# Loading the first 128 rows of w_out in one transfer, with two filler products fewer, in a fused attention and multiplicative-FFN kernel

## The chip, the cores and the metric

The kernel runs on one core of one Trainium2 chip. The metric is the device time of one execution in microseconds (us), as the median of several runs. A profile of one further execution is shown beside it. In the profile PE is TensorE (PEld its weight loads), DVE is VectorE, ACT is ScalarE, POOL is GpSimd and SP is SyncE, which issues nearly all DMAs here; L219 means line 219 of the kernel before.

## The reference, cut to what matters

```python
# attention: q, k, v are (8, 8, 576, 64) float32, g_norm is (64,)
kv  = einsum('bhsd,bhse->bhde', k, v)
out = einsum('bhsd,bhde->bhse', q, kv)
x   = out / sqrt(mean(out * out, -1) + 1e-6) * g_norm     # then to (4608, 512)
# FFN: w1, w2 (512, 1024), w3 (1024, 1024), w_out (1024, 512), all float64
a = x @ w1
b = x @ w2
h = a * b @ w3
y = h @ w_out                                             # (4608, 512) float32
```

The weights arrive as 64-bit floats. The kernel receives their bits as 64-bit integers and makes 32-bit floats of them on the chip.

## The kernel before

The last two matrix products are folded into one. Before any token is processed, the kernel computes w3 @ w_out (`w3o_sb`, 1024 by 512), so that the FFN ends in one product with `w3o_sb`. This fold is the first stage, about 78 us long, and the change lies in its first 14 us. After it, nine groups of 512 tokens go through attention, the two gates and the projection, with one level of a Strassen-Winograd scheme in the large products; the change does not touch that part.

**The fold.** It runs twice over eight chunks (`KF` = 8), once for each half of w3's rows. Chunk c consists of 128 columns of w3 (four blocks of 128 by 128 per half) and of the 128 rows of w_out that go with them. For each chunk PE turns the four blocks of w3 (`turn_w3`, L731, four 128x128 transposes into PSUM), ACT copies them to SBUF (L733), and `fold_chunk` (L747) adds four products of 128x128 by 128x512 to four PSUM banks. Every fp32 product appears in the profile as two records. For chunk 0 of the first half the products are split by columns of w_out: four products with columns 0 to 255, then, around the preparation of chunk 1, four with columns 256 to 511.

**Loads.** `load_next` (L212 to L239) loads one chunk into a tile `raw` of 1024 64-bit words per partition, 512 for w3 and 512 for w_out. There are four such tiles, and the first four chunks' loads are issued at the start, in order, on SP's queue. Chunk 0 is loaded in four DMAs of 256 KB each: two halves of w3 (two blocks each), then the two halves of w_out's columns. Every later chunk takes two DMAs of 512 KB.

**Conversion.** `conversion` turns a stretch of `raw` into fp32 in six instructions: on ACT the absolute value of the high word (L176) and the low word (L171), on DVE the sign (L181), the clamp (L185), the shift (L188) and the addition of both words (L193). Chunk 0 is converted in quarters of 256 words: quarters 0 and 1 are w3, quarters 2 and 3 are the two column halves of w_out. Chunk 1 is converted in halves of 512 words: first w3, then w_out. ACT and DVE work in the order in which this stage is written out (a manual schedule), and so do PE and SP; each engine waits in place for its operands.

**Filler products.** `keep_warm(n, small)` (L297 to L302) issues n products of 128x128 and `small` products of 16x16 of the identity matrix into a PSUM bank that nobody reads. It is called three times: `keep_warm(11)` at the very start, `keep_warm(1, 12)` between the turn of chunk 0 and its products, and `keep_warm(1, 13)` between the last product of chunk 0 and the first of chunk 1:

```python
            if c == 0:
                fold_chunk(0, c, range(NH), slice(0, N))
                fold_chunk(0, c, range(NH - 1), slice(N, DM))
                begin_next(lambda: turn_w3(0, 1))
                fold_chunk(0, c, [NH - 1], slice(N, DM))
                keep_warm(1, 13)
                continue
```

**Semaphores of the DMAs.** The DMAs share eight completion semaphores in turn, so a DMA that reuses one waits on its issuing queue until the DMA eight places earlier has landed. Two of the eight are first taken by the two small loads of g_norm on ACT's queue.

Of the kernel before, what the change touches and what calls it, by code (L numbers as in the profile page):

```python
# [22 lines left out]
def kernel(  # L23
# [37 lines left out]
    DM = H * D  # L61
# [23 lines left out]
    def bank(pool, tag):  # L85
        return pool.tile([P, 512], FP32, name=tag, tag=tag)
# [6 lines left out]
    def load_q(b, r):  # L93
        t = loaded["q", b, r] = inp.tile([P, 2, J * D], FP32, name="q_sb")
        nc.sync.dma_start(
            out=t, in_=q[b, 2 * r:2 * r + 2, 0:G, :].rearrange("h (p j) d -> p h (j d)", j=J)
        )

    def load_four(names, b, g):

        for name in names:
            t = loaded[name, b, g] = inp.tile([P, 2, JS * D], FP32, name=f"{name}_sb", bufs=1)
            src = dict(k=k, v=v)[name][b, 4 * g:4 * g + 4]
            src = src.rearrange("(r e) (p j) d -> (e p) r (j d)", e=2, j=JS)
            nc.sync.dma_start(out=t, in_=src)

    def load_q_left(b):
        if b % 2 == 0:
            q_left[b // 2] = inp.tile([P, H, D], FP32, name="ql_sb", bufs=1)
        nc.sync.dma_start(  # L110
            out=q_left[b // 2][(b % 2) * L:(b % 2 + 1) * L],
            in_=q[b, :, G:S, :].rearrange("h p d -> p h d"),
        )
# [95 lines left out]
    def raw_tile():  # L209
        return conv_pool.tile([P, 1024], w1.dtype, name="raw", bufs=RAW)  # L210

    def load_next():  # L212
        if len(raws) == len(todo):
            return
        what, i = todo[len(raws)]
        raw = raw_tile()

        def load(where, src):
            nc.sync.dma_start(out=raw[:, where].rearrange("p (c m) -> p c m", c=src.shape[1]), in_=src)  # L219

        if what == "w":
            for n, w in enumerate((w1, w2)):
                src = w[:, i * P:(i + 1) * P].rearrange("(c p) f -> p c f", p=P)
                load(slice(n * 512, (n + 1) * 512), src)
        elif what == "b":
            for h in range(2):
                src = w3[DF // 2:DF, (2 * i + h) * P:(2 * i + h + 1) * P]
                load(slice(h * 512, (h + 1) * 512), src.rearrange("(m p) f -> p m f", p=P))
        else:
            src = w3[0:DF // 2, i * P:(i + 1) * P].rearrange("(m p) f -> p m f", p=P)  # L230
            cols = w_out[i * P:(i + 1) * P, :].rearrange("p (c f) -> p c f", c=1)

            n = 1 if i else 2
            for h in range(n):
                load(slice(h * 512 // n, (h + 1) * 512 // n), src[:, h * NH // n:(h + 1) * NH // n, :])
            for h in range(n):
                f = slice(h * DM // n, (h + 1) * DM // n)
                load(slice(512 + f.start, 512 + f.stop), cols[:, :, f])
        raws.append(raw)  # L239

    converted = []
# [22 lines left out]
    def begin_next(between=None, at=1):  # L264

        if len(begun) < len(todo):
            begun.append(conversions(len(begun)))
            for n, (c, _) in enumerate((c, i) for c in begun[-1] for i in range(2)):
                if between is not None and n == at:
                    between()  # L270
                next(c)

    def end_next(load=True):
        for c in begun[len(converted)]:
            all_of(c)
        converted.append(len(converted))
        if load:
            load_next()
# [18 lines left out]
    def keep_warm(n, small=0):  # L297

        t = bank(ps_mm, "mm")
        for i in range(n + small):  # L300
            w = P if i < n else 16
            nc.tensor.matmul(t[0:w, 0:w], lhsT=ident[:, 0:w], rhs=ident[:, 0:w], start=True, stop=True)  # L302
# [424 lines left out]
    def turn_w3(half, c):  # L727
        t_ps = bank(ps_at, "at").rearrange("p (m f) -> p m f", m=NH)
        for m in range(NH):
            src = chunks[:, c, 0, m * P:(m + 1) * P]  # L730
            nc.tensor.transpose(t_ps[:, m, :], src, ident)  # L731

        nc.scalar.copy(place_w3(half, c), t_ps)  # L733
# [9 lines left out]
    def fold_chunk(half, c, ms, cols=slice(0, DM)):  # L743
        if c == 0 and 0 in ms and cols.start == 0:
            sums_ps[half] = [bank(ps_mm, "mm") for m in range(NH)]
        for m in ms:
            nc.tensor.matmul(  # L747
                sums_ps[half][m][:, cols], lhsT=w3T[half, c][:, m, :], rhs=chunks[:, c, 1, cols],
                start=(c == 0 and cols.start == 0), stop=(c == KF - 1),
                skip_group_check=(half == 0),  # L750
            )
            if c == KF - 1:
                nc.scalar.copy(w3o_sb[:, half * NH + m, :], sums_ps[half][m])
# [693 lines left out]
    with tc.manual_schedule(  # L1447
        engines={mybir.EngineType.DVE, mybir.EngineType.Activation, mybir.EngineType.SP}
    ):
        for _ in range(RAW):  # L1450
            load_next()
# [25 lines left out]
        for c in range(KF):  # L1477

            if c > 3:
                begin_next()  # L1480
            end_next()
            if c == 4:
                load_four("k", 0, 0)
                load_q(0, 0)
            elif c == 5:
                load_four("v", 0, 0)
                load_q(0, 1)
                load_q_left(0)
            if c == 0:
                fold_chunk(0, c, range(NH), slice(0, N))  # L1490
                fold_chunk(0, c, range(NH - 1), slice(N, DM))
                begin_next(lambda: turn_w3(0, 1))
                fold_chunk(0, c, [NH - 1], slice(N, DM))
                keep_warm(1, 13)
                continue
            cut = NH - 1 if c in (1, 5) else NH - 2
            fold_chunk(0, c, range(cut))
            if c < 4:
                begin_next(lambda: turn_w3(0, c + 1), 2)
            else:  # L1500
                turn_w3(*((0, c + 1) if c + 1 < KF else (1, 0)))
            fold_chunk(0, c, range(cut, NH))
# [8 lines left out]
        for c in range(KF):  # L1511
# [9 lines left out]
            if c < KF - 2:  # L1521
                if c + 1 < max(BEGIN):
                    begin_next()
                elif c < max(BEGIN):
                    begun.append(conversions(len(begun)))
                    for steps_of_w in begun[-1]:
                        next(steps_of_w)
                if c == max(BEGIN) + 1:
                    for steps_of_w in begun[len(converted)]:
                        next(steps_of_w)  # L1530
                    all_of(x_first)
                else:
                    end_next(False)
                if c in SPLIT:
                    t = turns[SPLIT[c]] = w3_by_dma(SPLIT[c])
                    next(t)
                    next(t)
                if len(raws) < FIRST:
                    load_next()
                if c == 2:  # L1540
                    for steps_of_w in begun[len(converted)]:
                        next(steps_of_w)
                elif c == max(BEGIN):
                    run(sum_w(0))
            elif c == KF - 2:
                end_next(False)
# [211 lines left out]
```

## Time and profile before

| | before |
|---|---|
| time, median of 3 runs | 738.72 us (738.55 to 739.32) |
| the profiled execution, its own time | 738.91 us |
| its span, first to last instruction | 736.8 us |
| PE busy | 731.3 us (99%) |
| DVE busy | 627.5 us (85%) |
| ACT busy | 381.1 us (52%) |
| granted TensorE clock | 1.00 |
| HBM read, written | 130.55 MB, 20.71 MB |

The time of an execution is the span and some 2 us around it. PE is busy nearly throughout, but the page's busy time of PE is modelled and covers waits inside a pipelined stream, so the time that an edit is worth must be read from the stage in which it lies, from the chain of waits and from the order of instructions there.

### The profile page before, as it was taken

The page shows a single profiled execution, that of the slowest core. Times are in us where ns is not written, and L with a number is a line of the kernel's source. Part 1 is how long each engine was busy: PE and PEld are TensorE (multiplying, and loading weights), DVE is VectorE, ACT ScalarE, POOL GpSimd, SP SyncE. Part 2 cuts the span into 40 slices and gives each one's busy share as a digit, 9 for nine tenths or more (in the row PEclk, how much of TensorE's full clock was granted, in tenths as well). Part 3 has the DMA queues.
Part 4 walks back from the last instruction along what each step waited for, and adds up shares of the span by engine and source line. Part 5 has one row for each costly group of instructions (what it writes and reads, how often), then busy time and mean ns, then how long its engine had stood idle before and what let it go on. Part 6 is the DMA issues. An engine that isn't in the chain of part 4 may idle for free.

```text
span 736.8 us, 16930 instructions
## 1 busy us (share of the span) xinstructions
PE 731.3 (99%) x6873; PEld 658.4 (89%) x6873; DVE 627.5 (85%) x1259; ACT 381.1 (52%) x660; POOL 23.1 (3%) x30
## 2 busy tenths in 40 slices
PE   8999999999999999999999999999999999999998
PEld 6455788888899999999999999999999999999998
DVE  7988898868879689969996899689879987997797
ACT  7888778315652676167517761675177313212321
POOL 0000000220001000000010001000001000000000
PEclk9999999999999999999999999999999999999999
DMA  8999925599999598869987988698748862565454
GB/s 309 355 338 249 285 94 154 157 329 274 326 299 321 172 286 245 277 159 276 259 275 166 302 237 278 157 299 242 253 115 217 221 209 87 187 214 158 135 196 142
DMA packets 138769, 170.44 MB, mean 231 GB/s; under 512 B 81220, under 2 KB 114116, under 8 KB 138692
## 3 DMA queue, kind: packets, MB, share of 16 engines
q1 hardware_dynamic: 136240, 155.02, 71.4%
q10 hardware_dynamic: 2452, 14.35, 5.8%
q8 instruction: 54, 0.88, 0.5%
q14 instruction: 23, 0.19, 0.1%
HBM read 130.55 MB, written 20.71 MB: 205 GB/s over the span
## 4 chain that ended last, share of the span: by engine, by line
PE 98%; DMA 1%; DVE 0%; SPq 0%; issue 0%; ACT 0%; DVEq 0%
PE mm L778 37%; PE mm L1330 23%; PE mm L1072 21%; PE mm L747 8%; PE at L778 3%; PE at L362 3%; PE mm L440 1%; PE at L440 1%; PE at L731 1%; DMA raw<-in_moe_w_out_dram 1%; PE at L1373 0%; PE at L459 0%; PE at L382 0%; PE mm L302 0%; SPq L219 0%; PE at L476 0%
## 5 line engine op out<-in xcount | busy, mean ns | idle before, releaser
L1121 ACT COPY slots<-mm 128x512 f32<-128x512 f32 x88 | 51.6, 586 | 127.3 <-PE mm L1330 83.1
L778 PE MATMUL mm<-xT,w_sb 128*128 128x256 f32 x432 | 99.3, 379 | 0.0
L778 PEld LDWEIGHTS mm<-xT,w_sb 128*128 128x128 f32 x432 | 81.4, 190 | 11.1 <-issue 0.5
L778 PE MATMUL mm<-xc,ws 128*128 128x256 f32 x328 | 74.4, 379 | 0.0
L778 PEld LDWEIGHTS mm<-xc,ws 128*128 128x128 f32 x328 | 62.3, 190 | 8.5
L796 ACT COPY slots<-mm 128x512 f32<-128x512 f32 x58 | 34.0, 585 | 69.5 <-PE mm L778 64.7
L747 PE MATMUL mm<-chunks,ab 128*128 128x512 f32 (+1 forms) x136 | 59.2, 573 | 0.3 <-DVE chunks L193 0.3
L1125 DVE TENSOR_TENSOR slots<-mm,slots 128x512 f32<-128x512 f32 x66 | 45.2, 685 | 16.3 <-PE mm L1072 15.9
L1122 ACT COPY slots<-mm 128x384 f32<-128x384 f32 x88 | 42.3, 481 | 25.0 <-PE mm L1330 22.1
L1072 PE MATMUL mm<-ws,w3o_sb 128*128 128x128 f32 x350 | 54.0, 275 | 0.0
L1330 PE MATMUL mm<-w3o_sb,ab 128*128 128x128 f32 x368 | 48.8, 276 | 0.0
L408 DVE TENSOR_REDUCE inv<-sq 128x8 f32<-128x512 f32 (+1 forms) x40 | 24.6, 629 | 26.9 <-ACT sq L407 26.9
L1072 PEld LDWEIGHTS mm<-ws,w3o_sb 128*128 128x128 f32 x350 | 46.4, 192 | 0.0
L1330 PEld LDWEIGHTS mm<-w3o_sb,ab 128*128 128x128 f32 x368 | 45.4, 192 | 0.5
L1330 PE MATMUL mm<-w3o_sb,raw 128*128 128x128 f32 x340 | 43.5, 275 | 0.0
L747 PEld LDWEIGHTS mm<-chunks,ab 128*128 128x128 f32 x136 | 24.0, 190 | 21.0 <-issue 17.9
L1330 PEld LDWEIGHTS mm<-w3o_sb,raw 128*128 128x128 f32 x340 | 40.7, 192 | 0.0
L778 PE MATMUL mm<-xT,ws 128*128 128x256 f32 x160 | 38.1, 381 | 0.0
L1126 DVE TENSOR_TENSOR slots<-mm,slots 128x384 f32<-128x384 f32 x66 | 36.3, 551 | 2.0 <-PE mm L1330 1.9
L778 PE MATMUL mm<-xc,w_sb 128*128 128x256 f32 x152 | 36.6, 384 | 0.0
L778 PEld LDWEIGHTS mm<-xT,ws 128*128 128x128 f32 x160 | 30.1, 190 | 4.3 <-ACT slots L796 0.2
L335 ACT COPY xT<-xn 128x1024 uint16<-128x1024 uint16 x26 | 30.2, 1167 | 3.5 <-DMA xn<-xT 3.5
(247 smaller groups left out, 1664.3 us busy)
## 6 DMA issues: line engine op xcount, KB each, us to landing
w3o_sb<-w_l SPq DMA_DIRECT2D x21, 896.0 KB, 6.2
w3o_sb<-w3o_l SPq DMA_DIRECT2D x18, 896.0 KB, 6.6
raw<-in_moe_w_dram SPq DMA_DIRECT2D x31, 512.0 KB, 7.8
raw<-w3o_l SPq DMA_DIRECT2D x15, 896.0 KB, 4.9
w3o_sb<-w3o_l ACTq DMA_DIRECT2D x14, 896.0 KB, 4.8
k_sb<-in_k_dram SPq DMA_DIRECT2D x16, 576.0 KB, 4.9
v_sb<-in_v_dram SPq DMA_DIRECT2D x16, 576.0 KB, 5.8
q_sb<-in_q_dram SPq DMA_DIRECT2D x32, 256.0 KB, 5.4
```

What stands on the lines that cost most here:

```text
L335: copy(words(dst), src)
L362: nc.tensor.matmul(ps[r * D:(r + 1) * D, :], lhsT=k_sb[rows, r, cols], rhs=v_sb[rows, r, cols], start=(j == 0), stop=(j == JS - 1),)
L408: adds["norm"] = nc.vector.tensor_reduce(out=inv[:, i], in_=sq.rearrange("p (h d) -> p h d", d=D), axis=AX.X, op=ALU.add)
L747: nc.tensor.matmul(sums_ps[half][m][:, cols], lhsT=w3T[half, c][:, m, :], rhs=chunks[:, c, 1, cols], start=(c == 0 and cols.start == 0), s ...
L778: nc.tensor.matmul(ps[:, u, :], lhsT=lhsT(a_name, u, c), rhs=rhs(b_name, c),  start=(u == 0 and c == 0 and new), stop=(c == chunks - 1), s ...
L796: copies.setdefault(name, []).append(nc.scalar.copy(t, ps))
L1072: nc.tensor.matmul(ps[place // 4][:, place % 4, :], lhsT=x, rhs=y, start=new and place // 4 not in seen, stop=True, skip_group_check=True,)
L1121: nc.scalar.copy(z[:, 0:4], ps[0])
L1122: return nc.scalar.copy(z[:, 4:7], ps[1][:, 0:3])
L1125: nc.vector.tensor_add(z[:, 0:4], ps[0], z[:, 0:4])
L1126: nc.vector.tensor_add(z[:, 4:7], ps[1][:, 0:3], z[:, 4:7])
L1330: nc.tensor.matmul(ps[place // 4][:, place % 4, :], lhsT=x[:, c, :], rhs=y[:, c, :], start=new and place // 4 not in seen, stop=(c == 1), ...
```

## The change

The load of chunk 0 still splits w3 in two, but brings w_out's 128 rows in one DMA of 512 KB, whole rows of 512 words, instead of two DMAs of 256 KB with half of each row. The last of the three `keep_warm` calls issues 11 small products instead of 13. The conversion of chunk 0 stays in quarters. Quarters 2 and 3 now both depend on the one DMA, so the separate DMA waits of ACT and DVE for quarter 3 are gone. One DMA fewer also moves every later DMA of this start by one place in the round of eight semaphores. Otherwise the instructions of each engine and their order are the same.

```diff
             n = 1 if i else 2
             for h in range(n):
                 load(slice(h * 512 // n, (h + 1) * 512 // n), src[:, h * NH // n:(h + 1) * NH // n, :])
-            for h in range(n):
-                f = slice(h * DM // n, (h + 1) * DM // n)
-                load(slice(512 + f.start, 512 + f.stop), cols[:, :, f])
+            load(slice(512, 1024), cols)
         raws.append(raw)
...
                 begin_next(lambda: turn_w3(0, 1))
                 fold_chunk(0, c, [NH - 1], slice(N, DM))
-                keep_warm(1, 13)
+                keep_warm(1, 11)
                 continue
```

## The prediction

> **What bounds the kernel now.** I read the page first: PE is busy 731.3 of 736.8 us and carries 98% of the chain that ended last, while 1% of the chain is a DMA of w_out. Then I asked for the chain in order of time, over the first 80 us.
>
> ```profile
> 1.75 5.11 DMA raw<-in_moe_w_out_dram
> 6.86 0.02 issue
> 6.88 0.45 ACT chunks L176
> 7.34 0.02 issue
> 7.36 0.30 DVE chunks L185
> ...
> 8.12 0.44 DVE chunks L193
> 8.55 0.14 issue
> 8.69 3.26 PE mm L747 x14
> 11.95 0.56 PE at L731 x4
> 12.51 0.43 PE mm L747 x2
> 12.95 0.97 PE mm L302 x28
> 13.91 2.77 PE mm L747 x6
> ```
>
> The columns are start, duration and what carried the chain. Until 8.69 us the end of the kernel hangs on the first half of w_out (issued at 1.75, landed at 6.86) and on its conversion. From 8.69 us on it is PE all the way: the waits of PE after 13 us are an empty list. So nothing later absorbs a shift; what this start loses or gains by its first product of chunk 1, at 13.84 us, the end does too.
>
> Next, DVE's part of the timeline (start, duration, line), to see what stands between the landing and 13.84 us.
>
> ```profile
> 6.37 0.42 DVE L193 CUSTOM_DVE_ANT_0 chunks<-chunks,ab 128x512 uint16<-128x512 uint16 x1
> 6.88 0.32 DVE L181 TENSOR_SCALAR ab<-raw 128x256 uint16<-128x256 uint16 x1
> ...
> 9.41 0.43 DVE L193 CUSTOM_DVE_ANT_0 chunks<-chunks,ab 128x512 uint16<-128x512 uint16 x1
> 9.75 0.46 DVE L181 TENSOR_SCALAR ab<-raw 128x512 uint16<-128x512 uint16 x1
> ...
> 12.98 0.69 DVE L193 CUSTOM_DVE_ANT_0 chunks<-chunks,ab 128x1024 uint16<-128x1024 uint16 x1
> ```
>
> DVE starts quarter 2 when the half lands (6.88) and then runs through quarter 3 and both halves of chunk 1 with no wait on a DMA, until 13.67 (12.98 and 0.69). The first product of chunk 1 starts at 13.84, right behind that. So DVE, not the fillers on PE, paces this stretch, and a later 6.88 moves 13.67 by the same amount.
>
> Last, the DMA view for the one issue at 2.33 us, and the wait list of tile raw up to 9.1 us.
>
> ```profile
> raw<-in_moe_w_out_dram SPq DMA_DIRECT2D x1, 256.0 KB, 5.2
> ```
> ```profile
>   DMA raw<-in_moe_w_out_dram: 0.9, 1
> ```
>
> The first column of numbers is the count, then the size and the us to landing: the second half lands at 2.33 + 5.2, by the landing record at 7.57, which is 0.71 us after the first. ACT waited 0.9 us for w_out, once: for the first half alone. The second half is not read before 8.03 (ACT) and 8.46 (DVE), so it has 0.46 us to spare.
>
> **The change, part by part.**
>
> *One transfer for two.* Quarter 2 now waits for all 512 KB. The trace's packet records give 84 ns for a packet of 2048 bytes and 159 ns for one of 4096 (half a row and a whole row; the 4096 ones are chunk 1's). Each of the 16 DMA engines carries 8 of the 128 rows. An engine now does 8 x 84 = 0.67 us for the first half; for whole rows it does 8 x 159 = 1.27 us. If its first packet starts when it does now, each engine ends 0.60 us later, and the last lands at 6.86 + 0.60 = 7.46. From the other side: both halves are in at 7.57, and whole rows save 8 x (168 - 159) = 0.07, which gives 7.50. I take 7.46, +0.60 us. The outer bounds are far. Below, DVE is busy with quarter 1 until 6.79 (6.37 and 0.42), so even an instant landing gains 0.09. Above, chunk 1's w_out, of the same size and shape, took 7.1 us from issue to landing; from 1.75 that is 8.85, +2.0. That row has 512 KB of chunk 1's w3 packed right ahead of it in the same rings, so I stay near the two halves' own rows.
>
> A rule of the Trainium skill can be weighed here (DMA: Bandwidth & Descriptors, "Rules for kernel authors"): coalesce many small transfers into one large one, since each pays a fixed cost, about 2 us by that page. Halves paying it in turn would be over 2 us apart; the trace's 0.71 us between their landings shows the cost overlapped, so by the trace there is nothing of it to save on the path.
>
> *What follows the landing.* Quarter 2's four DVE steps, quarter 3's four and chunk 1's eight keep their order, and move by 0.60. ACT has slack: its first step of chunk 1 waited 0.18 us for a DMA at 9.04, so ACT moves by only about 0.4 there. Chunk 1's loads (landed at 9.02 and 10.39 by the records) are not late, being issued earlier. PE's first product goes from 8.69 to 9.29, and the first of chunk 1 from 13.84 to 14.44.
>
> *One issue fewer on SP.* An issue is about 0.5 us of SP's time; the transfers behind it start that much sooner, or wait for another semaphore of the round. Chunk 2's w_out stood at 5.13 and chunk 3's w3 at 6.88 for reuse; in their new places they can go at about 3.8 and 5.13. Chunk 3's w_out, at 7.30 now, must wait for the one transfer, about 7.5. The DMA engines are over 0.9 busy from 6 us on and PE waits for none of these loads, so I cost this at nothing. If the cover were gone, 0.2 us of delay would be the price.
>
> *Two products fewer.* The 26 records of 16x16 start 25 ns apart, two records to a product, so two products are 0.10 us of PE. But the last filler starts at 13.735, DVE ends at 13.67 and the product starts at 13.84; the same hand-over at 8.54 to 8.69 took 0.15 us, so DVE alone would allow 13.82. The gain is 0.02 us, at most 0.10 if PE and not DVE set that start, as the chain has it. I take 0.02.
>
> Sum: +0.60 - 0.02 = +0.58 us. On the profiled execution, 738.91 (span 736.8 and 2.1 around it), that is 739.49. That execution is 0.19 above the median 738.72, from which it would be 739.30. I say 739.4. About 0.2%, or 1.48 us, is what a measurement of this kernel can tell from no change: my forecast lies well inside it.
>
> **The rivals.**
>
> *The transfer is no later than the half (no change, or a hair faster).* Between 3.75 and 4.75 us the DMA engines carry only some 200 GB/s against 375 to 400 later: some stand idle between the halves. One long transfer could fill these holes. Against it: the last engine sets the landing, and the records show that engine's two halves 0.71 apart, without a hole between. The gain is capped at 0.09 + 0.10 = 0.19 us: 738.5 to 738.9. Chance 0.16. That the split does nothing already is excluded: ACT went at 6.88, before the second half's 7.57.
>
> *TensorE's clock falls in the longer gap (slower).* PE now idles from 8.35 to 8.69 behind the fillers, and 0.85 us before 6.85. The first gap becomes 0.94 us, so between 6 and 9.3 us PE would have little but 16x16 products. If the clock were halved for half of the 3.26 us of products at 8.69, they would take 1.6 us more: with the 0.58, 740.9 from the median, and 742.6 if for all of them. It decides from the point where so thin a stretch counts as idle. For it: the fillers are the only PE work there. Against it: the granted clock reads 1.00 in every window that I asked for, through the 0.85 us gap too. The Trainium skill (TensorE: Matmul & The Clock Gate, "Why this matters for your kernels") wants no idle gap over about 3 us; by that rule 0.94 us leaves the clock alone, and no gap here is long enough to test it. Chance 0.10.
>
> *The whole transfer lands as late as chunk 1's row (slower).* At 7.1 us from issue to landing the shift would be +2.0 and the time 740.7. It needs an engine to get its share of descriptors later than it does now. Only a shift over 1.5 us passes the bound. Chance 0.09.
>
> **How the numbers follow.** The forecast, a shift of 0.3 to 1.1 us, has 0.60; its own range is 739.0 to 739.8. The rivals have 0.16, 0.10 and 0.09, and 0.05 is for what I don't see, split between the sides. Slower by over 0.2%: 0.10 + 0.09 and some of the rest and of the spread of the runs (0.8 us between the three shown), 0.23. Faster by over 0.2% has no mechanism, since the cap is 0.19 us: 0.04. Within: 0.73. The range starts at 738.4, below the capped gain, and ends at 740.9, at the near ends of both slower rivals.
>
> **What would show it.** Right: ACT's L176 of quarter 2 waits for w_out until about 7.5 instead of 6.88; DVE's L193 of chunk 1 ends near 14.27; PE's first 128x512 product follows at about 14.42; from there all is the same, shifted. The 16x16 records fall by four and the product after them still follows DVE. Wrong: quarter 2 starting near 6.9 (first rival), a granted clock under 1.00 in the first 20 us, or products at 8.69 over 379 ns each (second), or w_out landing after 8.3 (third). A shift at 14 us that the end does not show would break the reading that nothing later absorbs it.

## The result, and the profile after

| | before | after |
|---|---|---|
| median of 22 runs each | 738.59 us (738.09 to 739.56) | 741.06 us (738.79 to 742.83) |
| ratio to before | | 1.0026 (95% interval 1.0018 to 1.0034) |
| profiled execution, its span | 738.91 us, 736.8 | 741.13 us, 739.1 |

The changed kernel is slower by 0.26%, with an interval that lies wholly above 1. (The two medians alone give 1.0033; with two groups a median is unsteady, so I go by the ratio and its interval.) Its executions scatter over 4 us where those of before stay within 1.5. They form two groups, and the granted clock of TensorE tells most of them apart: in 12 of the 22 it reads 1.000, with a median of 739.74 us, and in 10 it reads 0.995 to 0.998, with a median of 741.25. Two of the twelve took 741.06 and 741.29 us all the same; neither was profiled, so why they are that long is not shown. The median of all, 741.06, lies at the lower edge of the second group and just above the top of the predicted range (by the ratio it would be 740.5, inside); my forecast of 739.4 is near the first.

The profiled execution is of the second group. This is its chain of waits, the answer to the one shown of before (L745 is before's L747, L729 is L731, L300 is L302):

```profile
1.75 6.52 DMA raw<-in_moe_w_out_dram
8.28 0.02 issue
8.30 0.44 ACT chunks L176
...
9.53 0.43 DVE chunks L193
9.96 0.14 issue
10.10 4.65 PE mm L745 x14
14.75 0.44 PE at L729 x4
15.19 0.43 PE mm L745 x2
15.62 0.87 PE mm L300 x24
16.48 2.77 PE mm L745 x6
```

Two things are longer. The transfer lands at 8.28 us, where in the kernel before the first half of w_out landed at 6.86: +1.42. And the 14 records of chunk 0's products take 4.65 us instead of 3.26: +1.39. The rest is what it was, less 0.10 for the fillers and 0.12 for the turn of chunk 1. So the first product of chunk 1 is 2.57 us late (13.91 to 16.48), and the span is 2.3 us longer.

DVE in the timeline (start, duration, line; the idle time before an instruction and what ended it in brackets), and the times that readers of tile raw waited for w_out up to 10.3 us (us in total, times):

```profile
6.27 0.42 DVE L193 CUSTOM_DVE_ANT_0 chunks<-chunks,ab 128x512 uint16<-128x512 uint16 x1
8.30 0.32 DVE L181 TENSOR_SCALAR ab<-raw 128x256 uint16<-128x256 uint16 x1 [1.61 <-DMA raw<-in_moe_w_out_dram]
...
14.38 0.69 DVE L193 CUSTOM_DVE_ANT_0 chunks<-chunks,ab 128x1024 uint16<-128x1024 uint16 x1
```
```profile
  DMA raw<-in_moe_w_out_dram: 4.1, 2
```

DVE now stands idle for 1.61 us before quarter 2, where it had 0.09. Its last step for chunk 1's w_out ends at 15.07 (14.38 and 0.69), 1.40 later than before. But the product starts only at 16.41, so in this execution PE and no longer DVE sets the pace there. With the hand-over of 0.15 us that before showed, DVE would have let it start at about 15.2 (an estimate). So of the 2.57 us some 1.4 belong to the landing and some 1.2 to PE. PE in the timeline, around its wait for w_out:

```profile
8.03 0.22 PE L1473 MATMUL at<-ident,g_row 1*128 1x1 f32 x1
10.10 4.65 PE L745 MATMUL mm<-chunks,ab 128*128 128x256 f32 x14 [1.84 <-DVE chunks L193]
```

Why is PE slow after that wait? The windows of this trace give, for stretches in us, the length, then busy time and instructions of PE, PEld, DVE, ACT and POOL, then the granted clock, DMA share and GB/s:

```profile
6.09:9.51 3.42, 1.95 (x33) 1.47 (x32) 1.37 (x5) 1.21 (x4) 0.00 (x0) 1.00 0.99 357
9.51:12.92 3.41, 2.82 (x7) 2.32 (x8) 3.05 (x9) 3.41 (x9) 0.00 (x0) 0.50 1.07 388
12.92:16.33 3.41, 3.41 (x39) 2.99 (x37) 3.19 (x8) 1.40 (x3) 0.00 (x0) 1.00 1.06 376
```

For 3.41 us, from 9.51 to 12.92, the clock is 0.50. These are the edges of the trace's own clock records. In the stretch of the same length before it lies the larger part of PE's wait for w_out, 1.26 of 1.84 us: its products end at 8.25 and start again at 10.10.

### The profile page after: what moved, and what is told of

Read it like the earlier page. It is cut to its first block, busy times and chain, and to the rows that moved or that the text cites. A ratio compares the mean times of both kernels' runs of the same rounds, so it can differ in the third digit from the quotient of the medians.

```text
span 739.1 us, 16920 instructions
## 1 busy us (share of the span) xinstructions
PE 732.8 (99%) x6869; PEld 660.6 (89%) x6869; DVE 629.0 (85%) x1259; ACT 380.4 (51%) x660; POOL 22.8 (3%) x30
## 4 chain that ended last, share of the span: by engine, by line
PE 98%; DMA 1%; DVE 0%; SPq 0%; issue 0%; ACT 0%; DVEq 0%
PE mm L776 37%; PE mm L1328 23%; PE mm L1070 21%; PE mm L745 8%; PE at L776 3%; PE at L360 3%; PE mm L438 1%; PE at L438 1%; DMA raw<-in_moe_w_out_dram 1%; PE at L729 1%; PE at L1371 0%; PE at L457 0%; PE at L380 0%; SPq L219 0%; PE at L474 0%; PE mm L300 0%
## 5 line engine op out<-in xcount | busy, mean ns | idle before, releaser
L745 PE MATMUL mm<-chunks,ab 128*128 128x512 f32 (+1 forms) x136 | 60.6, 586 | 1.8 <-DVE chunks L193 1.8
L745 PEld LDWEIGHTS mm<-chunks,ab 128*128 128x128 f32 x136 | 25.1, 198 | 22.8 <-issue 17.9
```

What stands on the lines that cost most here:

```text
L745: nc.tensor.matmul(sums_ps[half][m][:, cols], lhsT=w3T[half, c][:, m, :], rhs=chunks[:, c, 1, cols], start=(c == 0 and cols.start == 0), s ...
```

## The experiments

Each of the twelve was timed in 10 to 12 runs, with before beside it on the same chip, in four batches on three chips. Before's medians beside them were 738.73 (first four), 738.88 (next four), 738.64 (next two) and 738.70 us (last two). "Low" counts executions with a granted clock of 0.998 or less; of the 110 executions of before that were run beside these kernels none was low.

| kernel | median, us | ratio (95% interval) | low | median of the rest | of the low |
|---|---|---|---|---|---|
| the change | 741.06 | 1.0026 (1.0018 to 1.0034) | 10 of 22 | 739.74 | 741.25 |
| load alone | 740.91 | 1.0030 (1.0020 to 1.0041) | 6 of 10 | 739.92 | 741.96 |
| fillers alone | 738.83 | 1.0003 (0.9994 to 1.0012) | 0 of 11 | 738.83 | |
| change, more fillers | 740.12 | 1.0016 (1.0007 to 1.0025) | 0 of 11 | 740.12 | |
| halves swapped | 739.29 | 1.0008 (0.9999 to 1.0017) | 1 of 11 | 739.27 | 740.75 |
| two row halves | 740.84 | 1.0025 (1.0017 to 1.0034) | 6 of 11 | 740.26 | 741.26 |
| change, touch | 740.95 | 1.0029 (1.0018 to 1.0039) | 5 of 10 | 740.35 | 742.41 |
| before, touch | 739.24 | 1.0001 (0.9992 to 1.0010) | 0 of 11 | 739.24 | |
| before, no fillers | 738.71 | 0.9998 (0.9989 to 1.0006) | 2 of 11 | 738.69 | 740.40 |
| one transfer, 2 KB packets | 740.91 | 1.0021 (1.0012 to 1.0031) | 7 of 12 | 739.68 | 741.24 |
| w3 half by ACT | 738.84 | 1.0002 (0.9994 to 1.0011) | 0 of 11 | 738.84 | |
| w_out half by ACT | 739.76 | 1.0017 (1.0007 to 1.0028) | 5 of 12 | 739.47 | 741.36 |
| w_out whole by ACT | 741.24 | 1.0026 (1.0015 to 1.0037) | 7 of 11 | 739.54 | 742.05 |

**Which part of the change.** The load alone:

```diff
-                keep_warm(1, 11)
+                keep_warm(1, 13)
```

> The whole-row load alone, with the 13 fillers of before. Theory A (late landing of the whole transfer, and in part of the executions a fall of TensorE's clock in the gap that this makes): as the full change, 739.1 to 739.8 us where the clock stays at 1.000 and about 741.2 where it reads under 1.000, median 739.5 to 741.3. Rival B (the two fillers fewer thin out PE's work and let the clock fall): with 13 fillers the clock stays at 1.000 and the time is 738.7 to 739.8.

And the two fillers alone, on the kernel before:

```diff
-                keep_warm(1, 13)
+                keep_warm(1, 11)
```

> Two fillers fewer alone, w_out in halves as before. Theory A: no change, 738.5 to 738.7 us, clock 1.000 in all runs. Rival B: the clock under 1.000 in a good part of the runs and those some 1.5 us longer. If PE and not DVE set the first product of chunk 1: 0.10 us less, too little to be told.

The load alone does what the change does: 740.91 us, 6 of 10 low. The fillers alone do nothing that can be told, and none of their 11 executions was low. So the effect is that of the load, and the fall of the clock does not need the two fillers to be gone.

**Is it the clock, or only the landing?** The change, with five more 128x128 fillers where PE waits for w_out:

```diff
-        keep_warm(1, 12)
+        keep_warm(6, 12)
```

> The full change, with six instead of one 128x128 filler in the call ahead of chunk 0's products, about 1.1 us more of PE work in the gap. Theory A: the clock stays at 1.000 in all or nearly all runs, the part of the loss that goes with the clock is gone and the part that goes with the landing stays: median 739.3 to 740.0 us, and no run group around 741.2 with a lower clock. Rival (all of the loss is the late landing, the lower clock is hidden behind DVE): the same as the full change, about 741 us.

No execution was low, and the high group at 741.2 is gone: 740.12 us. In its trace w_out landed as late as with the change (8.12 us by the landing record), and the windows show a full clock:

```profile
6.06:9.47 3.41, 2.57 (x34) 2.21 (x34) 2.03 (x7) 1.75 (x6) 0.00 (x0) 1.00 1.00 353
9.47:12.88 3.41, 3.41 (x30) 2.97 (x26) 3.07 (x9) 3.41 (x8) 0.00 (x0) 1.00 1.06 390
```

So the loss has two parts. The late landing costs about 1.1 to 1.4 us where the clock stays full: 739.74 against 738.59 for the change, 740.12 against 738.73 here. (The second figure may hold a little of the fillers themselves: in the trace they and the small turn of g_norm behind them keep PE until 9.98 us, and DVE's quarter 2 is ready at 9.80.) The executions with half clock are 1.5 us longer than the others (741.25 against 739.74); the profile puts 1.39 us more on the 14 records, of which about 1.2 reach the next chunk. The two groups were sorted by the clock after the runs, so part of the 1.5 may be a still later landing; the split is an estimate, that there are two parts is shown.

**What decides the fall of the clock.** Two looks at it. The kernel before, with a thinner stretch of PE and no change of the loads:

```diff
-        keep_warm(1, 12)
+        keep_warm(1, 0)
```

> The kernel before, without the twelve 16x16 fillers in the call ahead of chunk 0's products; the loads are untouched. It makes the gap of PE ahead of 8.69 us about 1.3 us instead of 0.34 without any later landing. If a thin stretch of PE alone drops the clock: a good part of the runs reads under 1.000 and is 0.8 to 1.6 us longer than the rest, the rest at 738.7. If the 16x16 products do not count as work for the clock, or the fall needs more than 1.3 us: clock 1.000 and 738.5 to 738.8 us throughout.

Two of 11 executions were low, and these took 740.2 and 740.6 us against 738.69 for the rest. (The one that was profiled was not low. The first half of w_out landed at 6.07 us in it, so PE's wait ahead of the products was 0.58 us there and not the 1.3 that I had expected.) That none of the 110 of before was low suggests that the 16x16 fillers are of some use, though the median does not show it.

The other look goes through the traces. All clock records inside the kernels last a whole number of times 3.413 us: 3.41 and 6.83 us at half clock, and 730.45 or 733.87 (214 or 215 times) where it never falls. So the start of the first record gives a grid of 3.41 us, and its place differs from execution to execution, from 4.5 to 7.3 us. Only the trace of the fillers alone has no clock record. I worked out from the instruction records which share of each such stretch PE spent on products and transposes, leaving out the 16x16 ones (the small turn of g_norm, 0.22 us, is counted). The clock was halved after stretches with 0.39 (the change), 0.38 (load alone), 0.39 (2 KB packets), 0.37 (change, touch) and 0.34 (whole by ACT). It stayed full after 0.47 (two row halves) and after 0.56 or more in the others. Once halved, it stayed so for a second stretch after one with 0.43 (whole by ACT). Counted with the 16x16 products it doesn't sort: then 0.57 fell and 0.47 did not. The case of 0.47, with two row halves, has a wait of PE as long as that of the change, 1.92 us, but a grid that lies otherwise:

```profile
4.84:8.25 3.41, 2.61 (x39) 2.13 (x38) 1.55 (x5) 0.48 (x2) 0.00 (x0) 1.00 0.95 233
8.25:11.66 3.41, 1.59 (x8) 1.44 (x8) 2.89 (x10) 3.39 (x8) 0.00 (x0) 1.00 1.07 385
```

The second stretch here holds 1.82 us of the wait and ends in dense products; in the change's trace above, the stretch from 6.09 holds the thin 16x16 products and 1.26 us of the wait. So the length of the wait alone does not decide: more of it lay in a stretch after which the clock stayed full. As far as these traces show, it depends on how little full work the wait and the thin products leave in one stretch, and so on where the grid lies. This is a reading of thirteen traces, with a measure that was chosen after seeing them, and not an experiment: the grid can't be set.

**What a later landing costs by itself.** Before, with the column halves issued in the other order, so that quarter 2 must wait for both:

```diff
-            for h in range(n):
+            for h in reversed(range(n)):
                 f = slice(h * DM // n, (h + 1) * DM // n)
```

> As before, with the two column halves of w_out issued in the other order, so that quarter 2 waits for the second of two 256 KB transfers: the same bytes must be in before quarter 2 starts as with the whole rows, but in packets of 2048 bytes and two DMAs. If the bytes set the delay, quarter 2 starts at about 7.5 to 7.6 us instead of 6.88 and the time is 739.2 to 739.5 us, with a clock under 1.000 in a few runs at most. If late engines in any 512 KB of this start set it, quarter 2 starts as late as with the whole rows (about 8.3 us) in some runs and the runs scatter over 738.8 to 742 us as they do with the change.

This is a shift of the size that I had predicted for the change (+0.60), and in the profile it goes through to the end as the sum has it:

```profile
2.33 4.96 DMA raw<-in_moe_w_out_dram
7.30 0.45 ACT chunks L176
...
9.10 3.26 PE mm L747 x14
```

Quarter 2 starts at 7.30, 0.42 after before's 6.88; the 14 records of products start 0.41 later, and the span, 737.1 us, is 0.3 longer. The median is 739.29, 0.56 above 738.73, though the interval of the ratio begins at 0.9999, so the runs alone do not tell it from no change. All 512 KB were in by 7.3 us. The same bytes as whole rows took until 8.1 to 8.3 in the traces of the change, of the load alone and of the one with more fillers.

**Why whole rows land late.** Two DMAs again, but of 64 whole rows each:

```diff
-            load(slice(512, 1024), cols)
+            for h in range(n):
+                rows = slice(h * P // n, (h + 1) * P // n)
+                nc.sync.dma_start(out=raw[rows, 512:1024]..., in_=cols[rows])
```

> Chunk 0's w_out in two DMAs again, but each of 64 whole rows, so that quarter 2 needs both and every packet has 4096 bytes; 11 fillers. If the packets of whole rows (4096 bytes, of which a dozen took 0.5 to 1.3 us instead of 0.16 in the traces of the change) make the last engine late: quarter 2 starts at 8.0 to 8.3 us as with the one transfer, and the times are those of the change, 739.1 to 742.8 us in two groups by the clock. If it is the one 512 KB transfer, and not the packets' size: quarter 2 starts at about 7.3 to 7.5 us, and the time is about 739.3, as with the swapped halves.

The second landed at 8.19 and 6 of 11 were low. It isn't the number of DMAs, nor their size. Then one DMA with packets of 2048 bytes, made by exchanging the second and third quarters of the tile, so that the two halves of a row are not neighbours (the edits that move w3's second half and the conversion along are left out here):

```diff
-            load(slice(512, 1024), cols)
...
+                nc.sync.dma_start(
+                    out=raw.rearrange("p (c k f) -> p c k f", c=2, k=2)[:, :, 1, :],
+                    in_=w_out[0:P, :].rearrange("p (c f) -> p c f", c=2),
+                )
```

> The full change, one DMA for the 512 KB of chunk 0's w_out, but the two column halves go to two places of the tile that are not next to each other (the third and fourth quarter of the tile's layout are moved, the conversion reads them there), so that the one transfer is cut into packets of 2048 bytes. If the packet size makes the long packets: fewer of them, quarter 2 starts at about 7.3 to 7.6 us as with the swapped halves, about 739.3 us and the clock under 1.000 in few runs. If it is the whole 512 KB going out as one transfer in this place: quarter 2 at 8.0 to 8.3 us and the times of the change, around 741 us in two groups.

It landed at 8.08, and 7 of 12 were low: it isn't the size of the packets either. Third, a small DMA that visits every row first:

```diff
+        nc.scalar.dma_start(out=const.tile([P, 1], w_out.dtype, name="touch"), in_=w_out[0:P, 0:1])
         for _ in range(RAW):
             load_next()
```

> The full change, with a small DMA on ACT's queue at the start that reads one 8-byte word of each of the 128 rows into a tile that nobody reads. If the long packets are first visits to that memory, the touch takes them ahead: few packets over 0.45 us, quarter 2 at about 7.4 us, 739.2 to 739.6 us with the clock at 1.000 in nearly all runs. If they come from something else (the load of the queues, the size of the packets), a dozen long packets stay and the time is that of the change, around 741 us, or later by what the small DMA itself costs.

> The kernel before, with the same small DMA. If first visits are the cause, the late runs of before (739.1 to 740.4 us, about a third of them) go and the median falls by 0.1 to 0.3 us, to 738.4 to 738.6, which would be better than both kernels; more is not to be had, since DVE is busy until 6.79 us. Otherwise 738.7 to 739.2, the small packets costing something on the engines.

The small DMA had landed at 2.9 us, ahead of w_out's first packet at 3.6. With the change, w_out landed at 8.22 in the trace, and nothing got better; on before, nothing that can be told. So an earlier visit to each row does not help. The packet records show long packets: some packets of w_out that start between 3 and 6 us take 0.45 to 1.55 us instead of 0.16 (or 0.08 at 2048 bytes). Of those over 0.45 us there are 4 to 8 in the five traces with column halves on SP's queue, before's among them, and 9 to 17 in the six with whole rows there. With half of w3 or half of w_out on ACT's queue (the runs below) there are one and none. So the late landing goes together with more long packets. That they make it late is likely but not shown: the records do not name the engine of a packet. Why whole rows get more of them, I can't say. This stays open.

**Other queues.** Two tries to get w_out in sooner, on the kernel before, and one with whole rows. In the first, ACT's queue takes the second half of w3; in the others, ACT's queue takes the first half of w_out, or all of it, between the two loads of g_norm:

```diff
-            nc.sync.dma_start(out=raw[:, where]..., in_=src)
+            queue = nc.scalar if (what, i, where.start) == ("c", 0, 256) else nc.sync
+            queue.dma_start(out=raw[:, where]..., in_=src)
```

> The kernel before, with the second half of chunk 0's w3 issued from ACT's queue, so that SP's issues behind it, the first half of w_out first, go out 0.5 us earlier. In the trace of the kernel without fillers the half of w_out landed at 6.07 us and DVE set the pace from the first landing on (span 736.2 us). If so here: quarter 2 starts at 6.4 to 6.6 us behind DVE in nearly all runs, the late runs of before (739.1 to 740.4) go, and the median is 738.2 to 738.5 us, better than both kernels. If the two queues only share the DMA engines and the first half of w3 lands later for it: 738.7 to 739.5 us.

> The kernel before, with the first half of w_out issued from ACT's queue, between the two small loads of g_norm, at about 1.5 us, so that it does not stand behind w3 in SP's rings; the second half stays on SP. If a late first half is what makes the late runs of before (739.1 to 740.4 us): it lands before DVE has finished quarter 1 at about 6.5 to 6.8, the late runs go, and the median is 738.2 to 738.5 us. If sharing the DMA engines makes w3's halves land later, as in the run with w3's second half on ACT's queue (first landing at 4.08 instead of 3.57): 738.7 to 739.2 us.

> The full change, whole rows in one transfer and 11 fillers, with that transfer issued from ACT's queue at about 1.5 us. If the loss of the change is the late landing and what follows from it: quarter 2 starts at 6.6 to 7.4 us instead of 8.1 to 8.3, the clock stays at 1.000 in nearly all runs and the median is 738.6 to 739.4 us. If whole rows are late whatever the queue: quarter 2 at about 8 us and the times of the change, around 741 us in two groups by the clock.

None beats before. With w3's half on ACT's queue, the first half of w_out landed at 5.01, but the first half of w3 at 4.08 instead of 3.57, and DVE ran behind that. With w_out's half on ACT's queue, w3's second half landed at 6.09 instead of 5.12. With all of w_out there, both were late, w_out at 7.40 and w3's second half at 7.68; PE waited 3.53 us for its second turn, and the clock fell for two stretches:

```profile
4.72:8.13 3.41, 1.16 (x10) 0.92 (x9) 0.74 (x2) 0.43 (x2) 0.00 (x0) 1.00 1.01 370
8.13:11.55 3.42, 2.14 (x30) 1.86 (x30) 2.79 (x10) 2.46 (x8) 0.00 (x0) 0.50 1.05 386
11.55:14.96 3.41, 3.41 (x8) 2.71 (x9) 3.07 (x9) 2.83 (x6) 0.00 (x0) 0.50 1.07 373
```

In these traces what one transfer gained on ACT's queue another lost (w_out's half came at 5.92 instead of 6.86, w3's at 6.09 instead of 5.12), and whichever came last was waited for.

## Why the prediction was right or wrong

- *That the end hangs on the landing of w_out, then on DVE, then on PE, and that nothing later absorbs a shift:* right. From the first product of chunk 1 to the end it is 723.0 us before (736.8 less 13.84) and 722.7 after (739.1 less 16.41). Some 0.3 of the 2.57 us do not reach the end; where they go is not shown.
- *The landing at 7.46, +0.60:* wrong, and this is the first step that failed. It was 8.28 in the profile, +1.42, and 8.1 to 8.3 in the other traces of this load. The step said that each engine starts as now and ends 0.60 later, by 8 packets of 159 ns. It took the packets' usual duration for that of the last engine. A transfer leaves 16 landing records, one per engine: for before's first half the middle ones are at 5.5 us and the last at 6.86, for the whole rows they are at 5.9 and 8.28. So the middle of them moved by 0.4 us, less than my 0.60, and the last by 1.42. The sign stood in before's trace: the 200 GB/s from 3.75 us on, which I read as idle engines, come with a busy share of 0.84 up to 4.50 us; three packets of 1.0 to 1.55 us start at 3.90 to 4.35. The far bound, 7.1 us from issue to landing, held the 6.5 that came; I stayed too near the other end. The swapped halves, whose landing moved by 0.42, moved PE's products by 0.41, so the steps behind the landing were sound. That the range comes near the median is owed to the slower rivals, whose near ends set its top at 740.9; the sum itself did not lead there.
- *No cost for SP's moved issues:* right. Chunk 2's w_out went at 3.96 and chunk 3's at 8.29, by the issue records, and PE waited for neither.
- *The two fillers, 0.02 us, hidden behind DVE:* not contradicted at full clock. In the trace of the fillers alone the product starts at 13.99, 0.14 behind DVE's end at 13.85, and the times tell nothing so small. At half clock PE is late and they are worth their 0.10, which the chain shows as 0.97 to 0.87.
- *The fall of the clock, a rival with a chance of 0.10:* this is the second step that failed. I had its place and its price (1.6 us for half of the products; 1.39 came in the profile), but the point from which it decides was wrong. I took the gap as 0.94 us, which the late landing made 1.84, and held that the 0.85 us gap of before, at a clock of 1.00, spoke against a fall. A single gap is the wrong measure: it was 1.84 us where the clock fell and 1.92 with two row halves, where it did not; the traces sort by the work in a fixed stretch of 3.41 us. The rule that I cited (the Trainium skill, TensorE: Matmul & The Clock Gate, "Why this matters for your kernels": no idle gap over about 3 us) does not agree with these traces, where a gap of 1.84 us with thin products ahead of it was enough.
- *The chances:* 0.73 for a change within 0.2% was too sure; whether 0.26% is over that bound the interval, from 1.0018 on, leaves open. The two slower rivals were priced as strangers to each other, 0.10 and 0.09, while the one feeds the other: a landing 1.4 us late makes the gap after which the clock can fall.

## What to carry to other kernels

A transfer is in when the last of its 16 engines is: here the middle landing records were at 5.9 us and the last at 8.28. So price a landing by the slowest rows of the trace and by several executions, and not by bytes over the usual rate. If a first piece of a transfer releases work, keep it a transfer of its own: here half the columns came 1.4 us sooner than whole rows. And where a wait of PE grows, ask at once what that does to its clock, and whether what fills the wait is full-width work.

## What the runs showed of the hardware that I had not expected

- In these traces the clock changes only on a grid of 3.41 us, whose place differs between executions. It was halved for 3.41 us or twice that after a stretch with 0.34 to 0.39 of work other than 16x16 products, and not after 0.47 or more. That 16x16 products hardly count is read from this sorting and was not tried by itself.
- The same 512 KB land at 7.3 to 7.7 us as two column halves and at 8.1 to 8.3 as whole rows, all from SP's queue, whether in one DMA or two, and in packets of 4096 or 2048 bytes.
- Single packets of 2 to 4 KB take up to 1.55 us in this start, where their usual time is 0.08 to 0.16: 4 to 8 of them over 0.45 us with column halves on SP's queue, 9 to 17 with whole rows.
